# First mixture of two: experts taken in order of their counts, four of them in one common place

## The chip, the cores and the metric

The kernel runs on 1 core of one Trainium2 chip. The metric is device microseconds of that core. Engines are called as in the profile: PE (TensorE matmul), PEld (its weight load), DVE (VectorE), ACT (ScalarE), POOL (GpSimd), SP (SyncE, here the queue that issues plain DMAs).

## The reference, cut to what matters

A block-causal attention (4 x 8 heads, 576 x 64) makes 2304 rows of 512. Then come two mixtures of 8 experts each (512 to 1024 to 512). The change is in the first one; the second takes its output.

```python
def _moe_ref(x, w_skip, w_gate, w1, w2):
    skip_score = x @ w_skip
    do_compute = skip_score > 0
    out = x.copy()
    xc = x[do_compute]
    logits = xc @ w_gate
    e_idx = np.argmax(logits, axis=1)
    ...                                   # gate_w: softmax weight of the chosen expert
    for e in range(E):
        mask = e_idx == e
        h = np.maximum(xc[mask] @ w1[e], 0.0)
        y[mask] = gate_w[mask, None] * (h @ w2[e])
    out[do_compute] = xc + y
```

Each row goes to one expert or to none. With the inputs that `setup_inputs()` draws, the reference sends 460, 180, 122, 16, 10, 8, 8 and 2 rows to the experts 4, 3, 2, 5, 1, 0, 7 and 6.

## The kernel before, in words

The order of work is written by hand (`manual_schedule`). After the attention, the places of the second mixture that are known by then (two tiles of expert 0) are computed under the routing of the last batch: `up` (L393) and two calls of `down` (L439), woven with short steps at given output blocks f. At f = 3 of `up`, `last` takes the counts of all experts, and the list of rows per expert (`l1` in DRAM, 2304 seats for each expert) is read.

Then the first mixture runs as a row of "places" (L1217): a place is 128 rows of one expert. `tile1` (L1101) does it: `cut` transposes the gathered rows of the next place, `gemm1` (L1035) multiplies by the raw f32 w1 (32 matmuls 128x128 by 128 columns), `gemm2` (L1048) by w2 in two fp32r parts high and low (24 matmuls with 512 columns); the parts of the next expert's w2 are made in the same place (`split_steps`, L1152: ACT makes the high part, DVE and for one chunk POOL the low part). Between them stands the routing of the place before for the second mixture (`pending`: transposition, logits, two best experts, scatter to `l2`). SP loads 512 KB chunks, 4 of w1 and 4 of w2 for each expert, into 16 buffers (ST 8, ring 8), each as soon as its buffer is free.

The experts are visited in the order 0, 1, 2, a, 3, 4, 5, b, 6, 7. Every expert has one place; the fullest, a, is loaded a second time and gets 3 (`FULL`) more, the next, b, is loaded a second time and gets 1 (`NEXT`): 12 places and 10 loads of an expert. So expert 0 can be loaded while the counts are unknown. `fullest` (L965) finds a and b, `further` (L1000) makes the tables of their further places. What does not fit is done in a loop at the end (L1440), which does not run with these inputs.

Of the kernel before, what the change touches and what calls it, by code (L numbers as in the profile page):

```python
# [8 lines left out]
F32 = mybir.dt.float32  # L9
# [20 lines left out]
FULL, NEXT = 3, 1  # L30
# [16 lines left out]
def moe_kernel(ctx, tc, q, k, v, w_skip, w_gate, w1, w2, w_gate2, w_noise, noise, w1b, w2b, out):  # L47
# [54 lines left out]
    npad = fiota("npad", [P, 1], [[0, 1]], N, 1)  # L102

# [781 lines left out]
    with ExitStack() as bctx:  # L885
# [11 lines left out]
        with ExitStack() as ectx:  # L897
# [8 lines left out]
            for c in range(T0):  # L906
                raw_load(ST[c], w1, w2, 0, c)
# [8 lines left out]

            def split0(c):
                raw_split(ST[c], Q0, c, nc.scalar, nc.vector)
                raw_load(ST[c], w1, w2, 1, c)

            Q0 = Obj()
            Q0.w2h, Q0.w2l = Q2
            xg_pool = []
# [9 lines left out]
            def last():  # L933
                counted.extend(counts(C1, "n1"))
                late.L = L[B - 1][:, :, 9:25]
                late.nz = cst.tile([P, 5, E], F32, name="latenz")
                nc.vector.tensor_copy(late.nz, X[B - 1][:, :, D:W])
                late.inv = skip[B - 1]
                late.tok = tok_of(B - 1)
                xctx.close()  # L940
                xg = bctx.enter_context(tc.tile_pool(name="xg", bufs=1, side="right", reuse_waits="tile"))
                x = xg.tile([P, 6, D], F32, name="xg")
                XG.extend(x[:, i, :] for i in range(6))
                x_.append(x)
                nc.gpsimd.memset(x[:, 0:3, :], 0.0)
                lists.append(list_load(l1, 1, x[0:E, 3, :]))

            late, counted, XG, lists, x_ = Obj(), [], [], [], []
            up(WA, x0, h0, ((0, H0),), {1: begin, 2: lambda: go_on(3), 3: last, 4: lambda: split0(KC),
                                        5: lambda: split0(KC + 1), 7: lambda: split0(KC + 2)})  # L950
            tables = []

            def table():
                tok1, idx1, gate1, val1 = token_table(lists[0], 1, "t1", "s")
                nc.gpsimd.memset(x_[0][:, 3:5, :], 0.0)
                for e in range(2):
                    gather(xd, idx1[:, 0, e:e + 1], XG[e], N)
                inv1 = cst.tile([P, 1, E], F32, name="inv1")
                nc.vector.tensor_scalar(inv1, val1, -BIG, BIG, op0=OP.mult, op1=OP.add)
                tables.extend(t[:, 0, :] for t in (tok1, idx1, gate1, inv1))  # L960
                fullest()

            more, fuller = [], []

            def fullest():  # L965
# [7 lines left out]
                ni = cst.tile([P, 2], I32, name="fulli")  # L973
                nc.vector.tensor_copy(ni, ki[:, 0:2])
                fuller.extend(nc.values_load(ni[0:1, i:i + 1], engines=(mybir.EngineType.SP,), min_val=0, max_val=E - 1)
                              for i in range(2))
                nf = cst.tile([P, 2], F32, name="fullf")
                nc.vector.tensor_copy(nf, ki[:, 0:2])
                begun = cst.tile([P, E], F32, name="begun")
                own = cst.tile([P, E], F32, name="own")  # L980
                nc.vector.memset(begun, float(P))
                n = FULL + NEXT
                base = cst.tile([P, 2], F32, name="seatb")
                seat = cst.tile([P, n], I32, name="seats")
                for i, tiles_ in enumerate((FULL, NEXT)):
                    nc.vector.tensor_scalar(base[:, i:i + 1], nf[:, i:i + 1], float(R), posc, op0=OP.mult, op1=OP.add)
                    for t in range(tiles_):
                        c = i * FULL + t
                        nc.vector.tensor_scalar(seat[:, c:c + 1], base[:, i:i + 1], float((t + 1) * P), None, op0=OP.add)
                ctm = cst.tile([P, n, 2], F32, name="ctm")  # L990
                for c in range(n):
                    gather(l1, seat[:, c:c + 1], ctm[:, c, :], NROW)
                for i, tiles_ in enumerate((FULL, NEXT)):
                    nc.vector.tensor_scalar(own, e8, nf[:, i:i + 1], float(tiles_ * P), op0=OP.is_equal, op1=OP.mult)
                    nc.vector.tensor_tensor(begun, begun, own, op=OP.add)
                tokm, gatem, invm = (cst.tile([P, n], F32, name=nm + "m") for nm in ("tok", "gate", "inv"))
                idxm = cst.tile([P, n], I32, name="idxm")
                more.extend((begun, ctm, tokm, idxm, gatem, invm))

            def further():  # L1000
# [8 lines left out]
            down(WA, h0, 0, P, known[1][1][:, 0, :], known[1][2][:, 0, :], ep,  # L1009
                 {1: lambda: split0(KC + 3), 3: table})  # L1010
            tok1, idx1, gate1, inv1 = tables
            n1f, n1i = counted
            down(WA, h0, P, P, known[1][1][:, 1, :], known[1][2][:, 1, :], ep, {6: lambda: cut(0, 0, 0)})
        rp = bctx.enter_context(tc.tile_pool(name="rp", bufs=1, reuse_waits="tile"))
        ring = [ST[0:KC]] + [tiles(rp, f"r{i}", KC, F32) for i in range(2)]
        order = [0, 1, 2, fuller[0], 3, 4, 5, fuller[1], 6, 7]
        V = len(order)
        W1 = [ring[i % 3] for i in range(V)]
        places = []
        for j in range(V):  # L1020
            if j in (3, 7):
                for t in range(NEXT if j > 3 else FULL):
                    T = Obj()
                    T.j, T.work = j, t == 0
                    c = t + (FULL if j > 3 else 0)
                    T.gate, T.tok, T.idx, T.inv = (more[i][:, c:c + 1] for i in (4, 2, 3, 5))
                    places.append(T)
            else:
                T = Obj()
                T.j, T.work = j, True  # L1030
                T.gate, T.tok, T.idx, T.inv = (a[:, order[j]:order[j] + 1] for a in (gate1, tok1, idx1, inv1))
                places.append(T)


        def gemm1(j, e, half, between={}):  # L1035

            s = bank("s", 2 * j + half).rearrange("p (i n) -> p i n", i=4)
# [62 lines left out]

        def tile1(i):  # L1101

            T = places[i]
            j, k = T.j, i % 2
            work = split_steps(j) if T.work else {}
# [6 lines left out]
            turn, mm, first, second, third = pending(row1, k > 0)  # L1112
# [18 lines left out]
            extra(i)  # L1131
            o = gemm2(j, {4: third})
            pick("lo", 6)
            pick("load", 7, 6)
            if j == V - 1:
                for c in range(KC):
                    raw_load(ST[c], w1b, w2b, 1, c)
            finish(o, XG[i % 3], T.gate, T.tok, T.idx, T.inv)
# [13 lines left out]
        def split_steps(e):  # L1152

            def step(c):
                src = ST[c].rearrange("p (a d) -> p a d", a=2)
                h, l = (W2[e % 2][i][c - KC] for i in range(2))

                def hi():
                    nc.scalar.activation(h, src, AF.Copy)

                def lo():
                    (nc.gpsimd if c == NCH - 1 else nc.vector).tensor_sub(l, src, h.bitcast(F32))

                def load():
                    if e + 2 < V:
                        raw_load(ST[c], w1, w2, order[e + 2], c)
                    else:
                        raw_load(ST[c], w1, w2b, e + 2 - V, c)
                    if 1 <= e < V - 2:
                        raw_load(W1[e + 2][c - KC], w1, w2, order[e + 2], c - KC)  # L1170
                return {"hi": hi, "lo": lo, "load": load}
            return {c: step(c) for c in range(KC, NCH)}

        for c in range(KC):
            raw_load(W1[1][c], w1, w2, 1, c)
        for c in range(KC):
            raw_load(W1[2][c], w1, w2, 2, c)

# [37 lines left out]
        further()  # L1216
        for i in range(len(places)):  # L1217
            if i == len(places) - 2:
                settled.append(len(put_back))
            if i + 1 < len(places):  # L1220
                cut((i + 1) % 3, (i + 1) % 2, 0)
            if i + 2 < len(places):
                take(places[i + 2].idx, (i + 2) % 3)
            if i == 4:
                over = rest()
            tile1(i)
# [262 lines left out]
```

## Time and profile before

| | us |
|---|---|
| median of 3 runs | 952.01 (951.53 to 958.26) |
| the profiled execution | 954.42 |
| its span, first to last instruction | 952.6 |
| the 12 places, from 308.5 to 510.2 | 201.7 |
| PE busy / DVE / ACT / POOL over the span | 887.7 / 537.1 / 370.1 / 433.4 |

Times in the rows are microseconds from the start of the span. A busy PE is not PE at its peak, since matmuls are pipelined and their ends modelled; the starts of two matmuls that follow each other give their price. A plain f32 matmul is recorded as two instructions.

### The profile page before, as it was taken

How to read it: one execution, taken by the hardware profiler on the slowest of the kernel's cores; microseconds unless marked ns; L12 is line 12 of the kernel's file. 1: busy time of each engine (PE TensorE's matmuls, PEld its weight loads, DVE VectorE, ACT ScalarE, POOL GpSimd, SP SyncE). 2: the span in 40 equal slices, each digit the busy share in tenths (PEclk: the TensorE clock that was granted, in tenths of full speed). 3: DMA queues.
4: the chain of work that ended last, by engine and by line, in shares of the span. 5: the costliest groups of instructions: out<-in, count | busy, mean ns of one | idle time of the engine just before them, and what ended most of it. 6: DMA issues, size and time to landing. Idle time of an engine off the chain costs nothing.

```text
span 952.6 us, 16785 instructions
## 1 busy us (share of the span) xinstructions
PE 887.7 (93%) x6184; PEld 784.5 (82%) x6184; DVE 537.1 (56%) x1464; ACT 370.1 (39%) x664; POOL 433.4 (45%) x326
## 2 busy tenths in 40 slices
PE   6998998898789988899999999999999999999995
PEld 4777776676678877678788899999999999999994
DVE  4666756746355577255766464555546364555631
ACT  4565554544333433133433162242434233343400
POOL 1223254242226546535545341554828465570835
PEclk9999999988799999899997999999999999999998
DMA  6776378351154878338866272564645455560333
GB/s 99 155 148 153 82 153 137 75 119 34 45 207 141 279 277 262 49 112 265 264 199 200 46 226 67 142 123 124 143 104 123 98 141 105 135 144 1 27 34 43
DMA packets 161243, 125.77 MB, mean 132 GB/s; under 512 B 110784, under 2 KB 124864, under 8 KB 161152
## 3 DMA queue, kind: packets, MB, share of 16 engines
q1 hardware_dynamic: 136272, 100.34, 37.6%
q0 software_dynamic: 22448, 23.98, 14.8%
q8 instruction: 50, 0.82, 0.4%
q10 hardware_dynamic: 2432, 0.30, 0.2%
q14 instruction: 41, 0.34, 0.1%
HBM read 104.93 MB, written 23.51 MB: 135 GB/s over the span
## 4 chain that ended last, share of the span: by engine, by line
PE 77%; DVE 11%; issue 3%; ACT 3%; SPq 3%; DMA 2%; another core or an unknown queue 0%; POOLq 0%; DVEq 0%; POOL 0%; ACTq 0%
PE bank L403 22%; PE sums L635 6%; PE bank L1041 5%; PE bank L446 4%; PE bank L447 4%; PE bank L448 4%; PE bank L1285 4%; PE bank L1287 4%; PE bank L1286 4%; PE bank L607 3%; PE seta L556 2%; PE bank L387 2%; DVE atb L290 2%; PE bank L1057 2%; PE bank L701 2%
## 5 line engine op out<-in xcount | busy, mean ns | idle before, releaser
L1295 POOL DMA_INDIRECT out_dram<-y,toq x77 | 150.6, 1956 | 94.3 <-DVE y L1294 75.1
L403 PE MATMUL bank<-xh,w1h 128*128 128x296 f32 (+2 forms) x512 | 123.1, 301 | 0.0
L403 PE MATMUL bank<-xl,w1h 128*128 128x296 f32 (+2 forms) x512 | 122.1, 299 | 0.7 <-DVE xl L391 0.3
L403 PE MATMUL bank<-xh,w1l 128*128 128x296 f32 (+2 forms) x512 | 122.2, 300 | 0.0
L406 ACT ACTIVATE hh<-bank 128x296 fp32r<-128x296 f32 (+2 forms) x128 | 47.8, 413 | 149.2 <-PE bank L403 145.8
L635 PE MATMUL sums<-v,ptS 128*128 128x65 f32 x640 | 94.1, 283 | 9.9 <-remote 5.1
L407 DVE SCALAR_TENSOR_TENSOR hl<-bank,hh 128x296 fp32r<-128x296 f32 (+2 forms) x128 | 54.1, 459 | 77.1 <-ACT hh L406 74.0
L635 PEld LDWEIGHTS sums<-v,ptS 128*128 128x128 f32 x640 | 84.2, 199 | 12.2 <-remote 5.2
L403 PEld LDWEIGHTS bank<-xh,w1h 128*128 128x128 f32 x512 | 88.4, 191 | 0.9 <-ACT xh L390 0.2
L403 PEld LDWEIGHTS bank<-xl,w1h 128*128 128x128 f32 x512 | 87.8, 191 | 1.2 <-DVE xl L391 1.2
L497 ACT ACTIVATE ptS<-bank 128x384 f32<-128x384 f32 (+2 forms) x119 | 56.1, 511 | 82.8 <-PE bank L607 38.9
L403 PEld LDWEIGHTS bank<-xh,w1l 128*128 128x128 f32 x512 | 87.8, 191 | 0.0
L149 ACT ACTIVATE q2h<-st 128x1024 fp32r<-128x1024 f32 x32 | 62.2, 1945 | 61.6 <-PE bank L448 61.6
L202 POOL DMA_INDIRECT rows<-xd,t3x x35 | 35.6, 1018 | 86.0 <-PE bank L387 79.0
L194 POOL DMA_INDIRECT l<-ent,idxb x40 | 42.8, 1070 | 67.3 <-DVE C L185 33.3
L1285 PE MATMUL bank<-hh,q2h 128*128 128x336 f32 x224 | 72.3, 323 | 0.0
L1287 PE MATMUL bank<-hh,q2l 128*128 128x336 f32 x224 | 70.9, 317 | 0.0
L1286 PE MATMUL bank<-hl,q2h 128*128 128x336 f32 x224 | 70.8, 316 | 0.0
L152 DVE TENSOR_TENSOR q2l<-st,q2h 128x1024 fp32r<-128x1024 f32 x32 | 61.2, 1913 | 16.6 <-ACT q2h L149 16.6
L607 PEld LDWEIGHTS bank<-idf,P 128*128 128x128 f32 x320 | 36.4, 147 | 32.2 <-issue 19.1
L446 PE MATMUL bank<-q2h,hh 128*128 128x512 f32 x136 | 54.7, 402 | 0.0
L447 PE MATMUL bank<-q2l,hh 128*128 128x512 f32 x136 | 54.3, 399 | 0.0
(348 smaller groups left out, 1958.2 us busy)
## 6 DMA issues: line engine op xcount, KB each, us to landing
st<-in_moe_w_dram SPq DMA_DIRECT2D x124, 512.0 KB
r<-in_moe_w_dram SPq DMA_DIRECT2D x24, 512.0 KB
out_dram<-zero SPq DMA_DIRECT2D x19, 256.0 KB
kraw<-in_k_dram SPq DMA_DIRECT2D x60, 72.0 KB
qraw<-in_q_dram SPq DMA_DIRECT2D x60, 72.0 KB
v<-in_v_dram SPq DMA_DIRECT2D x64, 64.0 KB
xd<-Xe SPq DMA_DIRECT2D x2, 1024.0 KB
out_dram<-y,toq POOLq DMA_INDIRECT x77
```

The lines of the kernel that those rows point to most:

```text
L149: nc.scalar.activation(h, src, AF.Copy)
L152: on_low.tensor_sub(l, src, h.bitcast(F32))
L403: nc.tensor.matmul(s[i][:, :c1 - c0], a, part[:, c, c0:c1], start=st, stop=sp)
L446: nc.tensor.matmul(o[:n], a, wh, start=f == 0, stop=False)
L447: nc.tensor.matmul(o[:n], a, wl, start=False, stop=False)
L497: nc.scalar.activation(o, i, AF.Copy)
L607: nc.tensor.transpose(pt[:, c:c + P], U.P[:, h, c:c + P], idf)
L635: nc.tensor.matmul(o[:, h, t, :], U.T[h][:, c + j * P:c + (j + 1) * P], vb[:, j, h, :], start=j == 0, stop=j == t)
L1285: nc.tensor.matmul(o[:, :n], wh, a, start=f == 0, stop=False)
L1286: nc.tensor.matmul(o[:, :n], wh, b, start=False, stop=False)
L1287: nc.tensor.matmul(o[:, :n], wl, a, start=False, stop=f == FC - 1)
L1295: st = nc.gpsimd.indirect_dma_start(out=out.rearrange("n (a d) -> (n a) d", d=P), in_=y, in_offset=None, compute_op=OP.add, out_offset=bas ...
```

## The change

The whole first mixture waits for the counts. `ranking` (in `last`, at f = 3 of `up`) sorts the experts by their counts, SP reads all eight ranks into registers, and only then are the first expert's weights loaded. The four fullest get 4, 2, 1 and 1 places, one behind the other, so that each is loaded once. The other four share one place of 128 rows: each has 32 rows, and its matmuls write the 32 PSUM partitions of its part. They use no fp32r parts: `few_step(i)` multiplies by chunk i of each of the four experts (i = 0 to 3: w1, i = 4 to 7: w2), 8 matmuls of 128x32 by 512 columns in plain f32, and their steps stand in the middle of places 1 to 4 and in the common place, which is done between place 5 and place 7. There are 8 full places and 1 common one, and 8 loads of an expert. Tables come from 9 gathers on POOL in place of 4 and a plain load; the w2 parts of the first expert are made in its own first place.

```diff
-FULL, NEXT = 3, 1
+TILES = (4, 2, 1, 1)
+FEW = 32
...
-            for c in range(T0, NCH):
-                raw_load(ST[c], w1, w2, 0, c)
...
+            def ranking():
...
+                ni = cst.tile([P, E], I32, name="ranki")
+                nc.vector.tensor_copy(ni, ki)
+                rank.extend(nc.values_load(ni[0:1, i:i + 1], engines=(mybir.EngineType.SP,), min_val=0, max_val=E - 1)
+                            for i in range(E))
+                for c in range(NCH):
+                    raw_load(ST[c], w1, w2, rank[0], c)
...
+                for c in [0, 1, n - 1] + list(range(2, n - 1)):
+                    gather(l1, seat[:, c:c + 1], ctm[:, c, :], NROW)
...
+                for c, g in ((0, 0), (1, 1), (sum(TILES), 3)):
+                    gather(xd, idxm[:, c:c + 1], XG[g], N)
...
+            up(WA, x0, h0, ((0, H0),), {1: begin, 2: lambda: go_on(3), 3: last})
...
+            down(WA, h0, 0, P, known[1][1][:, 0, :], known[1][2][:, 0, :], ep, {4: further})
+            down(WA, h0, P, P, known[1][1][:, 1, :], known[1][2][:, 1, :], ep, {3: reached, 7: lambda: cut(0, 0, 0)})
...
+        fewbuf = [fewb, ST[KC:], ST[KC:], fewb, ST[KC:], ST[KC:], fewb, W1b]
...
+        def few_step(i):
+            if i in (0, KC):
+                sums[:] = [bank("s", 2 + half) for half in range(2 if i == 0 else 1)]
+            for half in range(2):
+                for g in range(P // FEW):
+                    cols = slice(g * FEW, (g + 1) * FEW)
+                    f = i if i < KC else 2 * (i - KC) + half
+                    nc.tensor.matmul(sums[half if i < KC else 0][cols], few[:, f, cols],
+                                     fewbuf[i][g][:, half * 512:half * 512 + 512], start=f == 0,
+                                     stop=f == (KC if i < KC else FC) - 1, skip_group_check=True)
...
+        splits = {0: lambda: split_steps(ST[KC:], 1, lambda c: few_chunk(1, c)),
+                  2: lambda: split_steps(fewb, 0, lambda c: few_chunk(3, c)),
+                  4: lambda: split_steps(fewb, 1, lambda c: few_chunk(6, c)),
+                  7: lambda: split_steps(fewb, 0, lambda c: None),
+                  8: lambda: split_steps(ST[KC:], 1, lambda c: raw_load(ST[c], w1, w2b, 1, c))}
...
+        def middle(i):
+            if i == 0:
+                few_rows()
+            if i == 1:
+                few_step(0)
+                seconds(1, fewb)
+                few_step(1)
+                load_few(2)
+            if i == 2:
+                few_step(2)
+                load_few(4)
+            if i == 3:
+                few_step(3)
+                few_relu()
+                seconds(2, fewb)
+                load_first(2, ST[0:KC])
+            if i == 4:
+                few_step(4)
+                load_few(5)
+            if i == 5:
+                load_few(7)
...
+        def few_place(i):
+            T = places[i]
+            turn, mm, first, second, third = pending(row1, i % 2 > 0)
+            gather(noise, T.idx, nz, N)
+            turn()
+            few_step(5)
+            for c in range(KC, NCH):
+                raw_load(ST[c], w1, w2b, 0, c)
+            mm()
+            first()
+            few_step(6)
+            seconds(3, fewb)
+            second()
+            few_step(7)
+            load_first(3, W1b)
+            extra(i)
+            third()
+            finish(sums[0], T.x, T.gate, T.tok, T.idx, T.inv)
...
+        load_few(0)
+        load_first(1, W1b)
```

`middle(i)` stands between `gemm1` and `gemm2` of place i. `seconds(j, buf)` loads the four w2 chunks and `load_first(j, buf)` the four w1 chunks of rank j; `load_few(i)` loads chunk i of the four experts of the common place; `few_turn` behind place 3 transposes their hidden rows.

## Rows read from the trace of the kernel before

**Rows 1.** The page: busy time of the engines, and the chain that ended last.
```profile
PE 887.7 (93%) x6184; PEld 784.5 (82%) x6184; DVE 537.1 (56%) x1464; ACT 370.1 (39%) x664; POOL 433.4 (45%) x326
...
PE 77%; DVE 11%; issue 3%; ACT 3%; SPq 3%; DMA 2%; another core or an unknown queue 0%; POOLq 0%; DVEq 0%; POOL 0%; ACTq 0%
```

**Rows 2.** Windows, one for each place: length, engines, PE clock, DMA share, GB/s.
```profile
308.50:325.00 16.50, 15.31 (x109) 13.38 (x108) 11.25 (x35) 6.62 (x11) 9.86 (x7) 1.00 0.86 268
...
376.20:398.20 22.00, 18.42 (x108) 14.56 (x107) 6.04 (x35) 3.01 (x7) 12.99 (x14) 0.84 0.35 74
398.20:412.90 14.70, 14.70 (x109) 13.37 (x107) 5.60 (x31) 2.90 (x7) 6.48 (x7) 1.00 0.25 38
...
495.60:510.20 14.60, 14.24 (x102) 12.61 (x101) 9.64 (x35) 5.98 (x10) 9.27 (x8) 1.00 0.52 144
sum 201.70, PE 186.50 PEld 161.72 DVE 123.62 ACT 71.76 POOL 107.25; mean PE 15.54 PEld 13.48 DVE 10.30 ACT 5.98 POOL 8.94
```

**Rows 3.** Chain of waits, 398 to 432: start, length, what ran.
```profile
398.64 1.79 PE bank L1041 x16
...
402.65 0.80 PE bank L1080 x8
...
423.67 1.86 DVE atb L290
```

**Rows 4.** Timeline of SP, 262 to 345.
```profile
296.24 0.34 SPq L362 DMA_DIRECT2D xg<-l  x1
...
302.36 17.73 SPq L131 DMA_DIRECT2D r<-in_moe_w_dram  x8
```

**Rows 5.** Line 975, the register loads of SP.
```profile
L975 SPq TENSOR_LOAD <-fulli x2: 276/376/475, 300.9 to 301.8; - x2
```

**Rows 6.** Timeline of POOL, 262 to 330 and 495 to 515.
```profile
293.82 1.16 POOL L194 DMA_INDIRECT l<-ent,idxa  x1 [0.30 <-issue]
...
303.08 1.01 POOL L202 DMA_INDIRECT ctm<-l,seats  x1 [0.30 <-issue]
304.39 1.01 POOL L202 DMA_INDIRECT ctm<-l,seats  x1 [0.30 <-issue]
...
507.33 0.99 POOL L202 DMA_INDIRECT fr<-xd,t6x  x1 [0.30 <-issue]
```

**Rows 7.** Timeline of PE around the first place, and behind the last.
```profile
306.65 0.63 PE L161 MATMUL bank<-idf,xg 128*128 128x128 f32 x4 [0.49 <-issue]
...
308.94 1.95 PE L1041 MATMUL bank<-xt,st 128*128 128x128 f32 x16
...
510.23 1.37 PE L387 MATMUL bank<-idf,fr 128*128 128x128 f32 x8 [0.39 <-DMA fr<-xd,t6x]
```

**Rows 8.** Window behind the places, columns as in rows 2.
```profile
512.80:522.90 10.10, 9.41 (x43) 9.11 (x44) 4.35 (x22) 1.78 (x5) 2.51 (x3) 0.50 0.81 298
```

**Rows 9.** Line 1041: instructions, ns min/median/max, starts, forms.
```profile
L1041 PE MATMUL bank<-xt,st x384: 270/275/356, 308.9 to 503.8; 128*128 128x128 f32 x192
```

**Rows 10.** Timeline of PE in 262.51:263.02: what has begun there.
```profile
262.50 0.70 PE L556 MATMUL seta<-kt,qt 64*128 64x512 f32 x2
```

**Rows 11.** Chain of waits, 255 to 530: the same four instructions.
```profile
262.57 1.06 PE seta L556 x4
```

**Rows 12.** Timeline of PE in 277.05:277.10: two parts of 64 columns.
```profile
277.04 0.28 PE L652 MATMUL sums<-v,ptS 128*64 128x65 f32 x2 [1.31 <-DVE Xo L643]
```

**Rows 13.** Timeline of PE, 262 to 345: a 64-column matmul among whole ones.
```profile
273.72 0.27 PE L619 MATMUL bank<-idf,P 128*64 128x128 f32 x1
273.83 1.90 PE L635 MATMUL sums<-v,ptS 128*128 128x65 f32 x16
```

**Rows 14.** DMA: issues in 308.5:510.2, and windows with w1, then mixed chunks.
```profile
st<-in_moe_w_dram SPq DMA_DIRECT2D x50, 512.0 KB
r<-in_moe_w_dram SPq DMA_DIRECT2D x22, 512.0 KB
...
324.00:328.00 4.00, 4.00 (x34) 3.77 (x33) 1.86 (x6) 0.80 (x2) 3.39 (x3) 1.00 1.02 391
340.00:344.00 4.00, 4.00 (x31) 3.63 (x30) 2.44 (x9) 0.60 (x1) 2.85 (x3) 1.00 0.88 312
```

More of the change, by code (lines that the diff above doesn't have):

```diff
@@ L944, in last @@
                 x_.append(x)
[L945 to L965, printed above, removed]
+                ranking()
+                nc.gpsimd.memset(x[:, 0:4, :], 0.0)
+            late, counted, XG, x_ = Obj(), [], [], []
+            more, rank = [], []
+            def ranking():
                 key = cst.tile([P, E], F32, name="key")
@@ L990, in fullest @@
[L990 to L994, printed above, removed]
+                nc.vector.memset(begun, 0.0)
+                for i in range(E):
+                    nc.vector.tensor_scalar(own, e8, nf[:, i:i + 1], float(TILES[i] * P if i < len(TILES) else FEW),
+                                            op0=OP.is_equal, op1=OP.mult)
@@ L995, in fullest @@
                     nc.vector.tensor_tensor(begun, begun, own, op=OP.add)
[L996 to L998 removed]
+                more[0] = begun
             def further():
@@ L1014, in moe_kernel @@
+            down(WA, h0, P, P, known[1][1][:, 1, :], known[1][2][:, 1, :], ep, {3: reached, 7: lambda: cut(0, 0, 0)})
         rp = bctx.enter_context(tc.tile_pool(name="rp", bufs=1, reuse_waits="tile"))
[L1015 to L1018, printed above, removed]
-        places = []
[L1020 to L1028, printed above, removed]
+        W1b, fewb = (tiles(rp, f"r{i}", KC, F32) for i in range(2))
@@ L1032, in moe_kernel, with load_first, load_second, load_few @@
                 places.append(T)
+        T = Obj()
+        T.j, T.x, c = None, XG[3], len(places)
+        T.gate, T.tok, T.idx, T.inv = (more[i][:, c:c + 1] for i in (4, 2, 3, 5))
+        dense = list(places)
+        places.insert(sum(TILES[:2]), T)
+        def load_first(j, buf):
+            for c in range(KC):
+                raw_load(buf[c], w1, w2, rank[j], c)
+        def load_second(j, buf, c):
+            raw_load(buf[c - KC], w1, w2, rank[j], c)
+        def load_few(i):
+            for g in range(P // FEW):
+                raw_load(fewbuf[i][g], w1, w2, rank[V + g], i)
@@ new lines, in few_rows, with few_relu, few_turn @@
+        def few_rows():
+            nc.scalar.activation(few[:, 0:KC, :].rearrange("p c n -> p (c n)"), transpose_rows(XG[3], 1), AF.Copy)
+        fewh = x_[0][:, 4:6, :]
+        def few_relu():
+            for half in range(2):
+                nc.scalar.activation(fewh[:, half, :], sums[half], AF.Relu)
+        def few_turn():
+            for half in range(2):
+                nc.scalar.activation(few[:, 4 * half:4 * half + 4, :].rearrange("p c n -> p (c n)"),
+                                     transpose_rows(fewh[:, half, :], half), AF.Copy)
@@ L1035, in gemm1 @@
         def gemm1(j, e, half, between={}):
-            s = bank("s", 2 * j + half).rearrange("p (i n) -> p i n", i=4)
+            s = bank("s", half).rearrange("p (i n) -> p i n", i=4)
             for i in range(4):
```

135 lines of the change are left out of this document (72 added, 63 removed).

## The prediction

> **What bounds the kernel now.** I read the page first: PE is busy 93% of the span and holds 77% of the chain that ended last [rows 1]. So a change counts by what it does to PE's row of work. Then the windows by place [rows 2]: 12 places take 201.7 us, 16.5 for one in which w2 is split and 14.7 for one in which it is not (398.20). The latter is PE alone: two halves of `gemm1` at 4 x 1.79 us, the logits 0.80, three transpositions, 24 matmuls of `gemm2` [rows 3]. A splitting place has some 1.8 us more, in which PE waits for DVE and ACT, the longest piece being one DVE instruction of 1.86 us [rows 3]. The place at 376.20 took 22.0 us, 7.3 more than its like: its clock column is 0.84, so half its stretch or less ran at the lower level (1.2 instead of 2.4 GHz) behind pauses of PE [rows 2]. Last the windows by DMA: w1 chunks land at 391 GB/s when nothing holds them back, a mix with w2 chunks at 312 [rows 14], and splitting places run at 268 [rows 2]; the 72 chunks of 201.7 us are 187 GB/s on the mean. Weights bound nothing for long today.
>
> **What is removed.** Four full places of twelve, and two of ten loads of an expert. Eight full places stay: three without splits (1, 3, 5), four with (0, 2, 4, 7) and the last, with splits but short (14.6 [rows 2]): 3 x 14.7 + 4 x 16.5 + 14.6 = 124.7; I add 1 for the routing of the last batch, which stands in places 2 to 5 as before. 125.7 us.
>
> **What is added on PE: the eight steps of the common place.** Each is 16 matmul instructions, since a plain f32 matmul is two: 192 matmuls of this form stand as 384 records [rows 9]. A row of 128 columns costs 1.79 / 16 = 0.112 us per instruction [rows 3], so 512 columns cost 4 x 0.112 = 0.447. If the four column parts run one after the other, a step is 16 x 0.447 = 7.15 us; if all four run at once, 1.79. The trace has no 128x32 matmul. Nearest is the pair of 64-row parts with 512 columns: the first instructions of both begin together (two begun at 262.50, the other two not before 263.02) [rows 10], and all four take 1.06 us [rows 11], 0.53 per round, where one after the other would be 1.79. Column parts are there only with 64 columns and a short moving side: two begin within 0.06 us of each other [rows 12], where whole matmuls are 0.11 apart. I take the row parts' round: 2 rounds per half, 4 x 0.53 = 2.13 us per step, 17.0 us for eight; 14.3 and 57.2 us are the ends.
>
> The Trainium skill (TensorEngine Tiling (Array Packing), Key Properties) says that changing the tiling mode drains TensorE, which speaks against 16 changes of mode here. The trace shows no such price: a 64-column matmul stands between whole ones at 0.11 us, their usual distance [rows 13]. By the rule, with the 0.27 us that this matmul takes from start to end as an estimate of one drain, the sum would be 16 x 0.27 = 4.3 us higher.
>
> Around the steps: 12 transpositions more (`few_rows`, `few_turn`) are 1.3 us. In the common place nothing covers the way from the end of place 5 through DVE's `finish` to the transposition of its rows: 1.5 us; transposition and logits are 1.2 and the tail of the routing, which has only two short steps above it, about 1. Together 5.0 us. Its matmuls have no splits, so ACT and DVE have no work there that could be late. PSUM: `gemm1` falls back to two banks, freed half a place before their next use; nothing.
>
> **What is moved: the head.** Today expert 0 is loaded ahead and place 0 begins when `down` ends, at 308.94 [rows 7]. Now three chains run from the counts (289 us).
>
> SP: eight register loads, the second 0.9 us behind the first, the first weight 0.6 behind that [rows 4, 5], so about 0.75 each and 6 us, with everything behind them on SP. Loads begin at about 297; 8 chunks (4.2 MB) at 312 GB/s take 13.4 us and land at 311, w1 by 303. Place 0 needs w1 at its start and w2 some 4 us in. Hidden, though only by the next chain.
>
> POOL: the last scatter to `l1` starts at 293.82 [rows 6] and has landed by 296.24, when the read that waits for it goes out [rows 4]. Then nine gathers at 1.31 us (1.01 and 0.30 [rows 6]) in place of four: to 308. They land some 2 us after their end (the last gather of the final rows ended at 308.32 and PE waited for it to 510.23, 1.9 us after 507.33 + 0.99 [rows 6, 7]): 310. `further` on DVE needs all nine; it stands in DVE's order behind f = 3 of the first `down`, so that the output rows of that `down` wait behind it, which costs PE nothing as the other bank is free. Its indices are out at 310.2; two row gathers and their landing: 313 and 314.5. `cut(0)` stands inside the second `down` ahead of its last output block, so PE stops at about 306 and goes on at 313; `cut(1)` follows at 314.5, and place 0 starts at 315.4. That is 6.5 us later than now. Behind these gathers on POOL wait the two output scatters, and behind their landing half of the buffers of the common place; its first step is a place and a half away, so hidden.
>
> The pause is 7 us, and today a shorter one (PE 4.71 us busy of 6.3) is followed by 10.1 us at clock 0.50 [rows 8], which cost half of that. I take 4 us for the restart; 0 and 5 are the ends.
>
> **Weights.** Each batch of four chunks waits until a step or a `gemm` frees its buffers. At 312 GB/s a batch of w2 takes 6.7 us and one of w1 5.4, and nearly all are issued a place ahead of their use. The exception is the fourth expert's w2: issued in the common place behind step 6, with four other chunks ahead of it on SP, it lands about 12 us later, and place 7 splits it 2 us after its start and needs the result 9 us in. ACT waits there with the hidden rows of `gemm1` queued behind: 3 us; 0 to 8 are the ends. The fourth expert's w1 comes behind that, in time for place 8.
>
> **Sum.** 6.5 + 4 + 125.7 + 17.0 + 5.0 + 3 = 161.2, and 3 for pauses of the kind that cost the two worst places of today some 9 [rows 2], 164.2, against 201.7: 37.5 us less. The profiled execution (954.42 us, span 952.6) would be 916.9; it stands 2.4 above the median of the three runs. The second mixture, PE-bound and unchanged, keeps its length. From the median of 952.0: 914 us. Own range: without lower clock, stall and further pauses, and with steps of 1.79, 902; with a stall of 8 and a drain at each step, 925.
>
> **Rivals.**
>
> *One after the other in pairs, 930 us.* If PE starts matmuls strictly in order, the second instruction of part 0 holds parts 1 to 3 back: only the second of one part and the first of the next overlap, 5 rounds of 0.447 per half, 4.5 us per step, 35.8 for eight. That is 18.8 more, less the 3 us of stall, which is then covered. For it: the program puts the two instructions of a matmul behind each other. Against it: both row parts begin together [rows 10]. The Trainium skill (TensorE: Matmul & The Clock Gate, Part 3) says this in its sentence that matmuls are strictly first in, first out in start and end; rows 10 speak against the rule for the row parts unless the two instructions were already mixed when they were issued.
>
> *Column parts do not overlap at all, 950 us.* Then 57.2 instead of 17.0: 40.2 more, less 4 of stall and of waits in the common place that are covered. The gain is gone within what can be measured. For it: two column parts read twice the moving data from the same partitions, which the row parts do not. Against it: the pair of rows 12.
>
> *Weights become the bound, slower.* 68 chunks (35.7 MB) must land between 297 and the start of the last place. The kernel is slower than now as soon as that start lies behind about 495, that is below 180 GB/s. At 160 GB/s the loads take 223 us and the time is 977. For it: the mean of today is 187, and no load may now begin before the counts. Against it: today's mean is set by free buffers, and places that do load run at 268 [rows 2].
>
> *It doesn't do what it says.* If a fifth expert had over 32 rows, the loop at the end would run and add a load of 4 MB and a place or more, 30 us and up: with counts of 10, 8, 8 and 2 it doesn't.
>
> **How the numbers follow.** Forecast 56%, pairs 20%, no overlap 13%, weights 5%, the loop 1%, a gain beyond the forecast's own range 5%. The range runs from 900 to 945: it holds the forecast with its own bounds and the pairs with theirs, and leaves out no overlap, weights and the largest gain. One per cent (9.5 us) is about what can be told from no change, as the three runs lie 0.7% apart. Faster by over 1%: forecast, pairs, larger gain, and a part of no overlap, 0.83; within 1%: 0.11; slower: 0.06.
>
> **What will show it.** Eight groups of 16 instructions of form 128x32, 1.06 us per half if the round is right, 2.2 if in pairs, 3.6 if not at all. PE idle from about 306 to 313 with a row gather as its releaser, and the clock at 0.50 behind it. First weights on SP at 297. The last place ending near 473. A wait of ACT for a DMA in place 7. Wrong would make it above all a step longer than 2.2 us, and then a batch of weights that lands after its step.

## The result, and the profile after

The changed kernel takes 917.68 us (median of 4 runs, 911.85 to 920.77) where the kernel before took 954.03 on the same chip (4 runs, 951.53 to 958.26): a ratio of 0.9607, 95% interval 0.9542 to 0.9673, 36.4 us less. The forecast was 914 with a range of 900 to 945. The profiled execution took 915.83 us (forecast 916.9), its span is 914.0.

The page of the kernel after, busy time of the engines and the chain that ended last; they answer to [rows 1]:
```profile
PE 845.0 (92%) x5912; PEld 740.1 (81%) x5912; DVE 491.4 (54%) x1360; ACT 340.2 (37%) x621; POOL 402.2 (44%) x314
...
PE 56%; DVE 4%; DMA 2%; issue 2%; ACT 1%; POOL 1%; SPq 0%; POOLq 0%; another core or an unknown queue 0%; ACTq 0%; DVEq 0%
```
PE is busy for 42.7 us less and still 92% of the span. (The shares of this chain add up to 66%: it was not followed back to the start.)

Windows of the kernel after, columns as in [rows 2]: the head from the end of the last `up` matmul to the first `gemm1`, places 0 to 5, the common place, places 7 and 8, and the sum:
```profile
297.40:320.90 23.50, 13.62 (x60) 11.01 (x58) 6.46 (x27) 1.53 (x4) 15.69 (x14) 0.84 0.68 207
320.90:338.60 17.70, 16.35 (x107) 14.50 (x107) 9.79 (x30) 7.06 (x12) 8.23 (x6) 0.93 0.80 242
338.60:357.00 18.40, 18.40 (x139) 14.35 (x138) 5.74 (x31) 2.79 (x7) 5.05 (x6) 1.00 0.77 274
357.00:374.10 17.10, 17.10 (x123) 13.75 (x122) 11.06 (x44) 6.93 (x13) 6.67 (x6) 1.00 0.90 288
374.10:395.40 21.30, 18.11 (x137) 14.87 (x135) 11.30 (x68) 4.89 (x11) 11.74 (x12) 1.00 0.72 234
395.40:413.60 18.20, 17.39 (x122) 14.07 (x123) 9.54 (x29) 7.18 (x13) 9.12 (x8) 1.00 0.85 240
413.60:432.90 19.30, 16.11 (x107) 13.57 (x105) 6.39 (x35) 2.90 (x7) 9.49 (x10) 1.00 0.80 230
432.90:440.00 7.10, 7.06 (x62) 2.79 (x63) 2.78 (x22) 1.22 (x4) 2.38 (x3) 1.00 0.49 115
440.00:456.50 16.50, 15.22 (x112) 13.38 (x110) 9.91 (x48) 6.79 (x11) 7.29 (x6) 1.00 1.05 397
456.50:473.10 16.60, 14.61 (x104) 12.84 (x102) 12.53 (x42) 6.09 (x10) 8.81 (x9) 1.00 0.52 177
sum 175.70, PE 153.95 PEld 125.14 DVE 85.50 ACT 47.38 POOL 84.48; mean PE 15.40 PEld 12.51 DVE 8.55 ACT 4.74 POOL 8.45
```
The kernel before, cut at the same two events:
```profile
295.40:308.90 13.50, 12.97 (x61) 10.08 (x60) 6.73 (x28) 3.15 (x5) 8.65 (x9) 1.00 0.67 239
308.90:510.20 201.30, 186.09 (x1273) 161.33 (x1271) 123.44 (x450) 71.76 (x126) 106.85 (x82) 0.97 0.66 210
```
So this section, from the end of `up` to the second mixture's first transposition, has 175.7 us where it had 214.8: 39.1 less, which is all of the gain (the stretch ahead of it is 2.0 us longer than before, the one behind it 1.5 shorter). Its two parts move against each other: the head costs 10.0 us more, the places 49.1 less. From here on "section" and "head" mean these two stretches.

The head, on three engines of the kernel after. POOL's timeline (the first and last of nine table gathers, then the first row gather), answering to [rows 6]:
```profile
298.38 1.07 POOL L207 DMA_INDIRECT ctm<-l,seats  x1 [1.89 <-DVE hl L412]
...
309.00 1.01 POOL L207 DMA_INDIRECT ctm<-l,seats  x1 [0.30 <-issue]
...
314.37 1.02 POOL L207 DMA_INDIRECT xg<-xd,idxm  x1 [2.54 <-issue]
```
DVE's timeline, where the tables are first read:
```profile
313.38 0.17 DVE L996 COPY tokm<-ctm 128x9 f32<-128x9 f32 x1 [14.38 <-DMA ctm<-l,seats]
```
PE's timeline, answering to [rows 7]: the row that ends the pause, the first half of `gemm1`, then the first two steps of the common place (place 1) with the `gemm1` ahead of them and the second matmul of the `gemm2` behind them, and the same two matmuls of place 8, which has no step.
```profile
317.88 1.09 PE L166 MATMUL bank<-idf,xg 128*128 128x128 f32 x4 [9.88 <-DMA xg<-xd,idxm]
...
320.90 3.20 PE L1076 MATMUL bank<-xt,st 128*128 128x128 f32 x16
...
343.90 3.82 PE L1076 MATMUL bank<-xt,st 128*128 128x128 f32 x32
347.65 1.92 PE L1051 MATMUL bank<-r,few 128*32 128x512 f32 x16
349.39 1.90 PE L1051 MATMUL bank<-st,few 128*32 128x512 f32 x16
...
351.56 0.40 PE L1091 MATMUL bank<-q2l,ht 128*128 128x512 f32 x1
...
461.44 3.82 PE L1076 MATMUL bank<-xt,r 128*128 128x128 f32 x32
...
465.33 0.40 PE L1091 MATMUL bank<-w2l,ht 128*128 128x512 f32 x1
```
PE stands 9.88 us and names the row gather. The tables land 4.4 us after the start of the last gather (309.00 to 313.38), the rows 3.5 after theirs (314.37 to 317.88). SP was not what held it; its first weight goes out at 297.65, as forecast (answering to [rows 4]):
```profile
297.65 4.01 SPq L136 DMA_DIRECT2D st<-in_moe_w_dram  x4
```

The steps: the two of place 1 begin 1.74 us apart. The line of these matmuls (answering to [rows 9]):
```profile
L1051 PE MATMUL bank<-r,few x64: 592/592/617, 347.7 to 439.4; 128*32 128x512 f32 x64
...
L1051 PE MATMUL bank<-st,few x64: 592/592/617, 349.4 to 434.9; 128*32 128x512 f32 x64
```
128 instructions in eight steps, each 0.59 us by itself; four begin together and a round of four takes 1.74 / 4 = 0.435.

### The profile page after: what moved, and what is told of

Same layout as the page of the kernel before. It is cut to its first block, busy times and chain, and to the rows that moved or that the text cites. A ratio compares the mean times of both kernels' runs of the same rounds, so it can differ in the third digit from the quotient of the medians.

```text
span 914.0 us, 16114 instructions
## 1 busy us (share of the span) xinstructions
PE 845.0 (92%) x5912; PEld 740.1 (81%) x5912; DVE 491.4 (54%) x1360; ACT 340.2 (37%) x621; POOL 402.2 (44%) x314
## 3 DMA queue, kind: packets, MB, share of 16 engines
q1 hardware_dynamic: 132928, 91.94, 36.4%
## 4 chain that ended last, share of the span: by engine, by line
PE 56%; DVE 4%; DMA 2%; issue 2%; ACT 1%; POOL 1%; SPq 0%; POOLq 0%; another core or an unknown queue 0%; ACTq 0%; DVEq 0%
PE bank L408 22%; PE bank L1381 4%; PE bank L1383 4%; PE bank L1382 4%; PE bank L1076 4%; PE bank L451 4%; PE bank L452 4%; PE bank L453 4%; PE bank L392 2%; DMA r<-in_moe_w_dram 1%; PE bank L1051 1%; PE bank L166 1%; PE bank L1090 1%; PE bank L1092 1%; PE bank L1091 1%
## 5 line engine op out<-in xcount | busy, mean ns | idle before, releaser
L154 ACT ACTIVATE q2h<-st 128x1024 fp32r<-128x1024 f32 x28 | 58.0, 2072 | 61.5 <-PE bank L453 61.5
L157 DVE TENSOR_TENSOR q2l<-st,q2h 128x1024 fp32r<-128x1024 f32 x28 | 56.3, 2012 | 15.6 <-ACT q2h L154 15.6
L199 POOL DMA_INDIRECT l<-ent,idxb x38 | 38.3, 1008 | 59.9 <-DVE C L190 28.8
L612 PE MATMUL bank<-idf,P 128*128 128x128 f32 x320 | 50.9, 300 | 3.3 <-DVE ptS L505 1.8
```

The lines of the kernel that those rows point to most:

```text
L157: on_low.tensor_sub(l, src, h.bitcast(F32))
L612: nc.tensor.transpose(pt[:, c:c + P], U.P[:, h, c:c + P], idf)
```

## The experiments

They ran in three groups on other chips than the result; the kernel before takes 923 to 926 us there, and each ratio is to it on the same chip. The first two runs are the two kernels as they are. The lines named are those of each kernel's own file.

**The changed kernel, and the kernel before, on these chips.** No edit.

> The changed kernel as it is, on the same chip as the three others of this call, so that they can be compared with it: 0.96 of the time of the kernel before, with a pause of PE of about 10 us ahead of place 0.

Measured: 893.42 us, ratio 0.9698 (0.9648 to 0.9748).

> The kernel before, unchanged, for its profile on this chip: the section of the twelve places has 201 to 204 us as on the first chip if the difference between the two chips (926 against 954 us) lies ahead of the first mixture or in the second one; a shorter section otherwise.

Measured: 920.6 us in one run. Windows of the kernel before here, head and places:
```profile
281.80:294.80 13.00, 12.84 (x61) 10.22 (x61) 7.07 (x27) 2.22 (x4) 8.98 (x9) 1.00 0.73 248
294.80:481.80 187.00, 180.75 (x1274) 158.94 (x1272) 124.11 (x451) 71.60 (x126) 108.23 (x82) 1.00 0.72 226
```
Windows of the changed kernel here, head and places, then its place 7:
```profile
281.80:306.10 24.30, 13.59 (x60) 10.99 (x58) 5.79 (x25) 0.98 (x2) 15.65 (x14) 0.82 0.69 199
306.10:452.30 146.20, 139.65 (x1002) 114.31 (x1002) 78.20 (x338) 46.17 (x87) 69.99 (x60) 0.98 0.85 264
...
417.50:437.80 20.30, 16.43 (x106) 13.88 (x105) 11.87 (x47) 6.80 (x11) 8.40 (x7) 0.92 1.02 390
```
The twelve places take 187.0 us at clock 1.00 here, 201.3 at 0.97 on the first chip: the place with lower clock that the prediction read there [rows 2] is missing, and PE is idle for 6.3 us of the places where it was for 15.2. The section goes from 200.0 to 170.5, 29.5 us less, not 39.1. So the change is worth some 30 us on these chips. The rest of the first chip's 36 fits the clock and the idle PE that the places of the kernel before show only there; why they do, no run shows.

**Part by part.** The loop over the four column parts goes outside that over the halves, so that four instructions of one part stand behind each other:
```
-            for half in range(2):
-                for g in range(P // FEW):
+            for g in range(P // FEW):
+                for half in range(2):
```

> The steps of the common place take the column parts one after the other: part outside, half inside, so that four instructions in a row belong to the same part. Theory A (PE looks ahead in its queue and starts what another part of the array can take): a step stays at 1.75 us and the time at that of the changed kernel, 918 us. Rival (matmuls start strictly in their order, and the four parts overlap only since they are issued in turn): only the last instruction of one part and the first of the next overlap, 13 x 0.43 = 5.6 us per step, 8 x 3.85 = 31 us more, less some 4 us of waits that are covered then: 945 us.

Measured: 893.78 us, ratio 0.9662 (0.9613 to 0.9710), section 170.0. PE's timeline in 333.93:333.97:
```profile
333.92 0.66 PE L1051 MATMUL bank<-r,few 128*32 128x512 f32 x4
```
Four instructions have begun within 0.05 us, and one part's own four, which share their columns, would be 0.43 apart each as whole matmuls are: they belong to four parts. The next step begins at 335.66, 1.74 us later. The first instructions of parts 1 to 3 do not wait for the three older ones of the part before them. The profile doesn't name the part of an instruction, but the distance of the four bears it out: 13 to 14 ns here and 7 in the changed kernel, with twice as many instructions of the older part in between. The Trainium skill (TensorE: Matmul & The Clock Gate, Part 3) says that matmuls are strictly first in, first out; the 1.74 us of this run speak against that for column parts, and the rival built on it falls.

**Whole columns.** The same matmuls with all 128 columns of the stationary operand, so that nothing can overlap; the common place's rows are then sums over its experts.
```
-   nc.tensor.matmul(sums[half if i < KC else 0][cols], few[:, f, cols],
+   nc.tensor.matmul(sums[half if i < KC else 0], few[:, f, :],
...
```

> Each matmul of the common place takes all 128 columns as its stationary side and writes all 128 rows, so nothing can overlap (the rows of the common place then hold sums over the four experts). Theory (the overlap of the four parts is worth three quarters of the steps, and they lie on PE's path): a step goes from 1.75 to 16 x 0.43 = 6.9 us, 8 x 5.1 = 41 us more, less up to 5 us of waits for weights that are covered: 954 to 959 us, the gain of the change gone. Rival (PE's steps stand in time in which PE would wait for weights anyway): 918 to 930 us.

Measured: 929.11 us, ratio 1.0038 (1.0012 to 1.0063). PE's timeline, the rows that answer to place 1 above:
```profile
327.35 3.82 PE L1076 MATMUL bank<-xt,st 128*128 128x128 f32 x32
331.00 7.03 PE L1051 MATMUL bank<-r,few 128*128 128x512 f32 x16
337.87 7.03 PE L1051 MATMUL bank<-st,few 128*128 128x512 f32 x16
...
344.97 0.40 PE L1091 MATMUL bank<-q2l,ht 128*128 128x512 f32 x1
```
A step is 6.87 us, 3.95 times 1.74. The section has 203.4 us, 32.9 more than the changed kernel, of 8 x 5.13 = 41 on PE; the rest is taken to have covered waits. Without the overlap of the four parts nothing of the gain is left.

**Short steps.** Six of the eight steps move 16 columns and not 512, with all weights loaded; what these matmuls compute is cut accordingly.
```
+   n = 512 if i in (0, KC) else 16
...
-   fewbuf[i][g][:, half * 512:half * 512 + 512], start=f == 0,
...
+   fewbuf[i][g][:, half * 512:half * 512 + n], start=f == 0,
```

> Six of the eight steps of the common place (all but the first of each sum) multiply only 16 of 512 columns, with all their loads and dependences kept; the rows of the common place lack the rest. Theory (the steps lie on PE's path at their price): each of the six falls from 1.75 to 0.3 us or so, 8 to 9 us less: 909 us. Rival (the weights of the common place set the pace): the steps then wait for their chunks and the time stays at 915 to 918 us.

Measured: 893.68 us, ratio 0.9633 (0.9588 to 0.9678), section 172.7. Waits of PE in 280:457:
```profile
PE bank L1052 <- DMA r<-in_moe_w_dram: 5.0, 3, 2.3
PE bank L1052 <- DMA st<-in_moe_w_dram: 3.8, 2, 2.3
```
The steps' time came back as 8.8 us of waits for weights and as stretches at a lower clock, two in the places (clock 0.72 in 350:362), so that the section is no shorter; that is what the rival expected:
```profile
414.00:426.00 12.00, 7.02 (x69) 6.65 (x69) 4.36 (x29) 1.53 (x5) 4.08 (x5) 0.57 1.01 296
```

**No batches.** The other side: six of the eight batches of weights are not loaded, the steps run whole on what lies in the buffers.
```
-   for g in range(P // FEW):
+   for g in range(P // FEW if i in (0, KC) else 0):
...
-   raw_load(fewbuf[i][c - KC], w1, w2, rank[V + c - KC], i)
+   if i in (0, KC):
+       raw_load(fewbuf[i][c - KC], w1, w2, rank[V + c - KC], i)
```

> Six of the eight batches of four chunks for the common place are not loaded (12.6 MB; its matmuls run in full on what the buffers held, so its rows are wrong). Theory A (the weights are hidden but for the fourth expert's w2): 0 to 3 us less than the changed kernel. Theory B (the weights set the pace of the places, and the steps merely stand in that time): 8 us or more less.

Measured: 893.14 us, ratio 0.9681 (0.9626 to 0.9736), section 168.3. Weights alone hold some 2 us of the section, and 0.7 of that is the head (23.6 for 24.3), which none of these batches touches.

**Neither.** Both edits.

> Left out: six of the eight batches of weights of the common place are not loaded, and the six steps on them run with 16 of 512 columns. Six steps of 1.74 us at full columns would be 10.4 us of PE, 16-column ones some 1 us. Theory: neither alone gained because each hides the other (with short steps PE waited 8.8 us for the weights and ran 30 us at half clock; without the weights the steps still stood in PE's row), so that both together give the 9 to 10 us back: section about 160 to 162 us against 170.5, ratio to the kernel before 0.957 to 0.960. Rival: the steps' own time is filled by something else, the clock or the splits of ACT and DVE; then the section is 166 us or more, as in the two single ones.

Measured: 886.98 us, ratio 0.9591 (0.9548 to 0.9634). Window of the places:
```profile
306.60:447.40 140.80, 130.77 (x1002) 114.32 (x1001) 79.62 (x335) 45.63 (x87) 70.15 (x60) 0.97 0.60 184
```
With its head of 23.9 us the section has 164.7: 5.8 us less than the changed kernel, more than either alone and less than the 9 or 10 expected. So step and batch cover each other in part: take one away and the other stands right behind. PE is busy for 8.9 us less here than in the changed kernel, so some 3 went to waits and to the lower clock (0.97), which these runs don't split further.

**Early rows.** The memset stands ahead of the table gathers on POOL; the tables of the first four columns come first, and the row gathers are issued on them; the others follow.
```
+   nc.gpsimd.memset(x[:, 0:4, :], 0.0)
    ranking()
-   nc.gpsimd.memset(x[:, 0:4, :], 0.0)
...
+   for nm, cols in (("m", [0, 1, n - 1, 2]), ("o", list(range(3, n - 1)))):
...
-   for c in [0, 1, n - 1] + list(range(2, n - 1)):
+   for c in range(a, a + n):
```

> The clearing of the row buffers goes ahead of the table gathers, the first two full places, the third and the common place get their table from the first four gathers, their rows are fetched before the other gathers, and the other tables are made in the middle of place 0. Theory (the ten table operations on POOL make the pause of 9.9 us of PE ahead of place 0): the rows of place 0 land at about 310 instead of 317.9, the pause falls to 2 or 3 us, the lower clock behind it to nothing or little: 7 to 11 us less, 907 to 911 us. Rival (the first expert's weights, which leave at 297.65 for 4.2 MB, are as late as the rows): PE waits for them instead, and the gain is under 3 us, 915 to 918.

Measured: 889.68 us, ratio 0.9622 (0.9580 to 0.9663). PE's wait for the first rows, and the first half of `gemm1`:
```profile
PE bank L166 <- DMA xg<-xd,idxm: 5.5, 1, 5.5
```
```profile
300.95 1.95 PE L1092 MATMUL bank<-xt,st 128*128 128x128 f32 x16
```
The pause falls from 10.7 (the changed kernel on these chips) to 5.5 us, as much as four gathers at 1.31 us; the clock is at half for 3.4 us (297.4 to 300.8) where it was for 10.2, and place 0 runs at 1.00; the section is 165.1. So four of the nine gathers made half of the pause, and the other half stays with five. The time is 4 us below that of part by part, which ran on the same chip (893.78), and not 7 to 11 us less, as expected; the intervals of the two ratios overlap.

**The second half of the first expert later.** As early rows, and w2 of the first expert is held back until the rows have landed.
```
-   for c in range(NCH):
+   for c in range(KC):
        raw_load(ST[c], w1, w2, rank[0], c)
...
+   nc.sync.dma_start(gate, XG[1][0:1, 0:8])
+   for c in range(KC, NCH):
+       raw_load(ST[c], w1, w2, rank[0], c)
```

> The early rows of the fourth experiment, and the four w2 chunks of the first expert leave only when the rows of place 1 have landed (a small transfer of these rows on SP stands ahead of them). Theory (the gathers for the tables and the rows land 3 to 5 us after their issue since 4.2 MB of weights stream at the same time): the table is there some 3 us and the rows some 4 us earlier, the pause of PE falls from 5.5 to 1 or 2 us, and w2 still comes in time: 3 to 4 us less than the fourth experiment, 8 to 10 less than the changed kernel. Rival (landing does not depend on the weights): the pause stays at 5.5 us, and place 0 waits for w2 on top: as the changed kernel or up to 4 us better.

Measured: 890.91 us, ratio 0.9641 (0.9594 to 0.9689), section 167.6: the pause is 4.5, and place 0 then waits for w2. The tables were read at 294.15, 4.2 us after the start of the fifth gather (289.96); with early rows alone it was 4.4 (288.36 to 292.80). Holding back w2 did not make them land sooner, and the 3 to 4 us that were expected from it did not come. But it didn't clear the way either, as w1 was still under way (266 to 378 GB/s from 288.5 to 292.7, 4 to 8 from 293.8 to 295.8).

**Both mended.** Early rows without a fifth gather ahead of the rows, and in the common place the second mixture's w2 chunks go out on SP behind the fourth expert's weights. The first line below is against early rows, the others against the changed kernel.
```
-   seek_places(1, 1)
...
-   for c in range(KC, NCH):
-       raw_load(ST[c], w1, w2b, 0, c)
    mm()
...
    load_first(3, W1b)
+   for c in range(KC, NCH):
+       raw_load(ST[c], w1, w2b, 0, c)
```

> Tables for the four seats that the first three row gathers need come first and no fifth gather stands ahead of the row gathers on POOL; and in the common place the four second-mixture w2 chunks (w2b) are issued on SP behind the fourth expert's w2 and w1 in place of ahead of them. Nothing is left out. My theory: the pause of PE ahead of the first place goes from the 5.5 us of the kernel with early rows to about 4, and ACT's wait for the fourth expert's w2 in place 7 (3.3 to 3.8 us in the changed kernel) falls below 1, so place 7 loses 2 to 4 us: 8 to 11 us less than the changed kernel, a ratio to the kernel before of 0.955 to 0.960 on this chip. Rival: the wait for w2 in place 7 was covered (PE was idle for only 1.3 us there), or comes back at the second mixture's first w2 use, which now has less lead; then only the pause counts, 5 to 6 us less than the changed kernel, a ratio of 0.961 to 0.963.

Measured: 892.16 us, ratio 0.9656 (0.9622 to 0.9690): a miss, no better than early rows alone. Windows: place 0, place 7, place 8:
```profile
301.10:321.70 20.60, 18.16 (x112) 16.10 (x111) 11.48 (x36) 7.06 (x12) 14.54 (x11) 0.85 0.77 223
415.00:430.10 15.10, 14.83 (x106) 13.01 (x105) 11.45 (x46) 6.57 (x11) 8.06 (x6) 1.00 1.03 389
430.10:446.70 16.60, 14.59 (x104) 12.82 (x102) 11.78 (x42) 6.08 (x10) 8.36 (x8) 1.00 0.71 243
```
Place 7 does lose its stall: 15.1 us for 20.3 in the changed kernel and 18.2 with early rows. Place 8 is longer here, 16.6 for 14.5 and 16.0. And the head gave nothing. PE's pause is 5.9, as the tables came no sooner though their last gather was issued earlier. POOL's timeline:
```profile
286.76 1.01 POOL L207 DMA_INDIRECT ctm<-l,seats  x1 [0.31 <-issue]
294.51 1.01 POOL L207 DMA_INDIRECT xg<-xd,idxm  x1 [6.74 <-issue]
```
DVE reads them at 293.53, 6.8 us after the start of the last gather. DMA queues in 286:293 (packets, MB, share of the 16 engines' time):
```profile
q1 hardware_dynamic: 932, 2.51, 96.4%
q0 software_dynamic: 128, 0.00, 3.5%
```
POOL's small packets (q0) trickle through seven microseconds in which the weights (q1) take 96% of the engines. And place 0 took 20.6 us at clock 0.85 where early rows had 18.1 at 1.00, behind a pause only 0.4 us longer; the clock was at half to 303.8 and again, behind a wait of 2.4 us for a part of w2, from 317.5 to 320.9. These 2.5 us and the 0.6 of place 8 took back the 3.1 of place 7.

**Filled pause.** 40 matmuls that nobody reads stand in PE's order ahead of the transposition of the first rows.
```
...
+   o = bank("s", 2)
+   for t in range(40):
+       nc.tensor.matmul(o, h0[0][:, t % FC, 0:P], WA.w2h[t % FC // 2][:, t % 2, :], start=True, stop=True)
...
```

> The changed kernel with 40 more matmuls of 128 columns, whose result nobody reads, in PE's order ahead of the transposition of the first gathered rows: they fill part of the pause of about 10 us and nothing waits for them. My theory: the half clock behind the pause (313 to 323.5 in the changed kernel) is the price of the pause itself and costs 3 to 4 us; if PE works on until shortly before the rows land, the first gemm1 half takes 1.8 us in place of 3.2 and place 0 is 2 to 4 us shorter, at the same landing of the rows. Rival: the clock falls all the same, because what is left of the pause is still long enough, or falls later in the places; then the section from the end of the last up to the second mixture has the same length within 1 us.

Measured: 890.69 us, ratio 0.9635 (0.9585 to 0.9684). PE's timeline, then the windows of head and places:
```profile
292.02 9.32 PE L997 MATMUL bank<-w2h,hh 128*128 128x512 f32 x40
302.66 0.63 PE L166 MATMUL bank<-idf,xg 128*128 128x128 f32 x4 [1.31 <-DMA xg<-xd,idxm]
...
304.61 1.95 PE L1082 MATMUL bank<-xt,st 128*128 128x128 f32 x16
```
```profile
281.60:304.60 23.00, 21.53 (x99) 17.25 (x98) 5.75 (x25) 0.98 (x2) 15.44 (x14) 1.00 0.69 209
304.60:449.70 145.10, 137.76 (x1003) 112.53 (x1001) 78.97 (x335) 46.21 (x87) 69.21 (x61) 1.00 0.85 266
```
The clock stays at 1.00, and the section has 168.1 us, 2.4 less than the changed kernel's 170.5: 1.3 in the head, 1.1 in the places. Of the places, only place 0 stands behind the restart, 16.9 us for 17.5; the other 0.5 us are differences of later places. So the restart costs some 2 us.

**Two places fewer, nothing else.** The kernel before without the second and third further place of the fullest experts; their rows are not processed.
```
-   for t in range(NEXT if j > 3 else FULL):
+   for t in range(1):
```

> The kernel before without the second and third further place of the fullest expert (no loads and no splits belong to them; 204 rows are left without their expert). It prices a removed place. Theory (a full place costs its 14.7 us of PE, and the half clock and the pauses of the worst one go with it): 29 to 37 us less than the kernel before. Rival (the loads of the experts behind them need that time): under 25 us less, since PE then waits for weights.

Measured: 896.26 us, ratio 0.9712 (0.9657 to 0.9767), 27 us less than the kernel before, some 13.5 per place; the section has 168.3, (200.0 - 168.3) / 2 = 15.8 per place. That lies between the 29 to 37 us expected and the rival's 25. (The time behind the section is longer than in the kernel before, 441.8 us for 437.0, where the second mixture gets other rows.) So a place is worth 13 to 16 us here, and two of them nearly as much as the whole change, which removes four and adds the common one.

## Why the prediction held, step by step

The section was forecast at 164.2 us beside 201.7, both counted from 308.5; in the two traces it is the head's 10.0 more and 152.2 of places, 162.2, beside 201.3. That the sum is only 2.0 us off is in part luck: terms that came out 3.5 and 2.1 us higher stand against three that came out 2.7, 3.1 and 1.8 lower.

| term | forecast | first chip, after |
|---|---|---|
| head | +6.5 | +10.0, of it 1 us for transpositions at half clock |
| restart in place 0 | 4 (0 to 5) | 3.20 - 1.95 = 1.3 (2.3 with the head's part) |
| eight steps | 17.0 (14.3 to 57.2) | 8 x 1.74 = 13.9 |
| around the common place | 5.0 | 7.1 - 3 x 1.74 + 1.3 = 3.2 |
| eight full places, stall, pauses | 125.7 + 3 + 3 | 152.2 - 1.3 - 13.9 - 3.2 = 133.8 |

**Steps.** Right in kind, 3 us too dear in size: column parts overlap almost fully (3.95 of 4), and the round is 0.435 us and not the 0.53 of the row parts [rows 11]. The end of the range at 1.79 us per step was the better guess; the 13.9 us lie just below it. That it rested on this is shown by whole columns (+35.7 us between the medians, for 36 forecast for that rival). Pairs is refuted by part by part. Where the prediction was wrong is the change of mode, which it put at nothing from [rows 13]. From the second half of `gemm1` to the second matmul of `gemm2`, place 8 takes 3.89 us without a step (461.44 to 465.33); place 1 takes 7.66 with two, less 2 x 1.74 that is 4.18. With whole columns, where the mode stays, the same way is 17.62 less 2 x 6.87 = 3.88. So going into the steps and out again costs 0.3 us. There are six such pairs, since two steps stand together in place 1 and two in the common place: an estimate of 1.7 us, in the last two rows of the table. The Trainium skill (TensorEngine Tiling (Array Packing), Key Properties) states a drain at a change of mode, without a price; the trace agrees that the change costs something, but not the 4.3 us that the prediction estimated for it.

**Head.** The chain was right (nine gathers, tables, row gather, cut, with PE waiting for the row gather), its size 3.5 us short, most of it in the landings. Issue to landing was taken from a gather at the end of the mixture [rows 6, 7], and in the head it is 3.5 us from the start of a row gather and 4.4 from that of the last table gather. Early rows shows that the chain sets the pause: with five gathers ahead in place of nine it is 5.2 us shorter.

**Restart.** Half as dear as taken (some 2 us, not 4), inside the bounds. The clock was at half from 313.3 to 323.5, about as long as in [rows 8], but PE stood idle for the first 4.6 us of it.

**Weights.** Hidden, as forecast: without six batches the section changes by some 2 us. What the prediction didn't see is how close behind they stand: short steps turned into 8.8 us of waits. The one stall named is there. ACT waited 3.3 us for w2 in place 7 of the first trace:
```profile
ACT w2h L1144 <- DMA r<-in_moe_w_dram: 3.3, 3, 1.8
```
PE lost 1.3 us by it there, and some 5 on the other chip (20.3, against 15.1 with the loads reordered, of which 2 come back in place 8): within the 0 to 8 given.

**Pauses.** Larger than the 3 us on the first chip: places 3 and 5 have 3.2 us of idle PE each (21.3 - 18.11 and 19.3 - 16.11), in place 3 the longest piece, 1.79 us, in front of the transposition at 395.46, behind the hidden rows' eight transpositions. For that piece and those of place 5 the profile names no releaser but "issue". In the same kernel on another chip they are not there: place 3 takes 18.6 us, and no wait of PE in places 1 to 5 is longer than 0.3 us. So the order of work alone doesn't make them; their cause stays open.

**The base.** The term that carried more than the prediction said was not one of the change. 201.7 us held a place of 22.0 at lower clock [rows 2] and other idle time of PE, which the sum replaced by ordinary places. On another chip the same places take 187.0, and the gain is 30 us. The forecast of 37.5 us less holds for the chip of the trace and not for the others; the ratios lie between 0.96 and 0.97.

## What to carry over

Small products with few rows each can share TensorE in column parts at little loss: four experts of 32 rows took a quarter of the time with a part of the columns each (1.74 us a step) that they took with all columns (6.87), in plain f32, and 0.3 us for each way into such steps and out. When such a change makes an address come later, count the gathers that stand ahead of the first one needed, and look for a row of their landing that has as much traffic beside it as there will be. And before a gain is summed from windows, read their clock and their idle time: a low-clock place in the trace of before is not a gain of the change.

## What the hardware did that was not expected

Column parts ran ahead of older matmuls of other parts: four instructions of four parts began within 0.05 us although each part's four stood together in the order, and the step stayed at 1.74 us.

The landing of small indirect gathers varied from 4.2 to 6.8 us after the start of the last one, and the kernel that issued them earliest had the longest. Their packets shared the engines with weights at 96% there, but no kernel ran them without any weights beside, so the cause is argued and not shown. In the changed kernel DVE reads the tables at 313.38, when the weights have landed as well (331 GB/s on the mean of 301:313, 3 in 313:316).

Two pauses of PE of 5.5 and 5.9 us, in kernels nearly alike up to there, were followed by a first `gemm1` half of 1.95 us at full clock in one (early rows) and by one at half clock in the other (both mended):
```profile
301.12 3.23 PE L1091 MATMUL bank<-xt,st 128*128 128x128 f32 x16
```
The granted clock fell in both, at 297.4 and at 297.0. In the one it was back at 300.8, just ahead of `gemm1`, in the other only at 303.8. So what a pause of this length costs behind it is not steady: nothing in the first half of `gemm1` of the one, 1.3 us in that of the other.
